# Adding the gates' logits one step later, and the last tile's product with v in both column halves, in an attention and expert kernel

## The chip, the cores and the metric

The kernel runs on one core of one Trainium2 chip. The metric is device time in microseconds (us): the median of the runs shown. All times in a trace are us from the start of the span of one profiled execution. The engines are TensorE (PE, with its weight loads PEld), VectorE (DVE), ScalarE (ACT), GpSimd (POOL) and the DMA queues, here issued by SyncE (SP). Each engine runs its instructions in the order in which the program gives them, so an instruction that waits holds up all that stand behind it on its engine.

## The reference

There are two blocks: attention in which each query keeps only its 32 best keys, and a mixture of experts with one expert per token and a capacity of 80 tokens for each.

```python
# q, k, v: (8, 8, 576, 64) float32
scores = scale * np.matmul(q, k.transpose(0, 1, 3, 2))
kth = np.partition(scores, -32, axis=-1)[..., -32:-31]
scores = np.where(scores >= kth, scores, -1e9)
attn = np.exp(scores - scores.max(-1, keepdims=True))
attn = attn / (attn.sum(-1, keepdims=True) + 1e-9)
x = np.matmul(attn, v)            # then to (4608, 512): tokens x heads*dims
...
logits = x @ w_gate               # (4608, 8)
expert_idx = np.argmax(logits, axis=1)
gate_w = softmax(logits)[expert_idx]
# for each expert e: of its tokens keep the 80 with the largest gate_w
out[tok_idx] = gate_w[tok_idx, None] * (np.maximum(x[tok_idx] @ w1[e], 0) @ w2[e])
```

## The kernel before

**Tiling.** The 64 pairs of batch and head are taken two heads at a time: 32 head pairs n, of which four (hp = 0 to 3) make a batch. The 576 queries of a head are four full tiles of 128 (t = 0 to 3) and a last tile of 64 (t = NF = 4). A full tile of a head pair is two units, one for each head. The last tiles of both heads share one unit, head 0 in partitions 0 to 63 and head 1 in 64 to 127. So a head pair has 9 units, and there are 288 in all.

**The order.** The order of all instructions of the attention is written out by hand, in `run`. Its `step(i)` issues the work for unit i and for the units a few steps before it:

- DVE: the search for the 32nd best score. `parts` finds candidates (L241); `search` takes the best of them (L252, L260) and, after y, the exact threshold (L266, L269). y is the product of scores and signs (L264), on DVE for even units and on POOL for odd ones. A step also holds the reciprocals of finished row sums (`over`, L351), which are the last of its DVE work from the letter list (L459).
- ACT: the sign of scores less a bound (L257), the mask for odd units (L278; POOL makes it for even ones, L280), the exponential (L323, L325), the division by the row sums (`divide`, L360), and copies of scores out of PSUM (L233).
- PE: scores of a unit four steps ahead (`front`, L226), transposes with the mask added (`turn_w`, L316 and L321), and the product of the weights with v (`back`, L339), in the order that the lower part of `step` gives.

**The product with v.** `back` multiplies the transposed exponentials wT of a unit with vb, which holds v and a column of ones, so that the 65th column is the row sum. The output is 128 rows of PSUM. Each matmul fills 64 of them, from one half of the array's columns (r = 0 or 64); the two halves of a full tile take the same v. For the last tile the rows number 64 for each head. Here both heads' products go to rows 0 to 63, in different columns of the PSUM tile:

```python
for r in range(0, m, TL):
    r0 = r if t < NF else TL * h
    nc.tensor.matmul(cc[r : r + TL, o], lhsT=wT[:, ..., r0 : r0 + TL], rhs=vb[:, c, h, :], ...)
```

**The gates' logits.** When a head pair is done, `norm` stores its rows to memory (L369, L371), transposes them (L201), copies the result (L377), multiplies with two heads' rows of w_gate (L382), copies the product out of PSUM (L389), and adds it on DVE to the logits of the batch (L392). Only the first head pair of a batch needs no addition. `norm` is a generator: each `yield` ends what one step issues of it. The yield's value says whether the next part needs PE (1), in which case it is put off while a step has other PE work, or not (0). Generators are advanced at the end of a step (L505), so what they put on DVE stands behind that step's search and reciprocals and ahead of the next step's. After the last head pair of each second batch `gates` follows (L403 to L426), in four parts of one step each: maximum, exponential on ACT, the chosen expert, and its weight, kept in R.

After the attention, `route` picks the tokens of each expert from R, and `finish` computes the experts.

Of the kernel before, what the change touches and what calls it, by code (L numbers as in the profile page):

```python
# [14 lines left out]
Act = mybir.ActivationFunctionType  # L15
# [12 lines left out]
def kernel(  # L28
# [11 lines left out]
    nc = tc.nc  # L40
    B, H, S, D = q.shape
# [7 lines left out]
    scale = 1.0 / math.sqrt(D)  # L49
    P = 128  # L50
    HP = H // 2
    NP = B * HP
    NF = S // P
    TL = S - NF * P
# [94 lines left out]
    class Attention:  # L149
# [178 lines left out]
        def back(self, n, t):  # L328

            wT, cc = self.w.pop((n, t))  # L330
            vb = self.vb[n % len(self.vb)]
            m = P if t < NF else TL
            for h in range(2):
                o = slice(2 * P + h * (D + 1), 2 * P + (h + 1) * (D + 1))
                j = h if t < NF else 0
                for c in range(NK):
                    for r in range(0, m, TL):
                        r0 = r if t < NF else TL * h
                        nc.tensor.matmul(cc[r : r + TL, o], lhsT=wT[:, j * NF + c if c < NF else 2 * NF + j, r0 : r0 + TL],  # L339
                                         rhs=vb[:, c, h, :], start=(c == 0), stop=(c == NF))  # L340
            self.w[n, t] = cc

        def over(self, n, t):


            m = P if t < NF else TL
            sums = self.w[n, t][:m, 2 * P : 2 * P + 2 * (D + 1)].rearrange("p (h d) -> p h d", h=2)[:, :, D]
            z = self.z[:m, n % NP, t, :]
            if self.lean:
                nc.vector.tensor_scalar(z, sums, EPS, None, op0=Alu.add)  # L350
            nc.vector.reciprocal(z, z if self.lean else sums)  # L351

        def divide(self, n, t):
            m = P if t < NF else TL
            if t == 0:
                self.xn[n] = self.rows.tile([P, NK, 2, D], F32, name="xn", tag="xn")
            cc = self.w.pop((n, t))
            for h in range(2):
                o = 2 * P + h * (D + 1)
                nc.scalar.activation(self.xn[n][:m, t, h, :], cc[:m, o : o + D], Act.Copy, scale=self.z[:m, n % NP, t, h : h + 1])  # L360

        def norm(self, n, b, hp, bi, nb, cs=range(NK)):


            xn = self.xn[n].rearrange("p c h d -> p c (h d)")
            one, cols = bass.ds(b, 1), slice(hp * P, (hp + 1) * P)
            full = [c for c in cs if c < NF]
            if full:
                nc.sync.dma_start(xv[one, : NF * P, cols].rearrange("o (c p) d -> p (o c) d", p=P), xn[:, :NF, :])  # L369
            if NF in cs:  # L370
                nc.sync.dma_start(xv[one, NF * P :, cols].rearrange("o p d -> p o d"), xn[:TL, NF:, :])  # L371
            yield 1
            ps = self.four()[:, :2, :].rearrange("p j c -> p (j c)")
            at = slice(cs[0] * P, min(S, cs[-1] * P + P))
            self.turn_in(ps, xn, cs)
            xT = self.xT
            nc.scalar.copy(xT[:, at], ps[:, at])  # L377
            yield 1
            lp = self.four()[:, 0, : NK * E].rearrange("p (c e) -> p c e", e=E)
            for c in cs:  # L380
                for r in range(0, P, TL):
                    nc.tensor.matmul(lp[r : r + TL, c, :], lhsT=xT[:, c * P + r : c * P + r + TL], rhs=wg[:, hp, :],  # L382
                                     start=True, stop=True)
            if bi == 0 and hp == 0:
                self.lg = self.small.tile([P, nb, NK, E], F32, name="lg", tag="lg", bufs=2)
            cs = slice(cs[0], cs[-1] + 1)
            lg = self.lg[:, bi, cs]
            part = lg if hp == 0 else self.small.tile([P, NK, E], F32, name="part", tag="part", bufs=2)[:, cs]
            nc.scalar.copy(part, lp[:, cs])  # L389
            yield 0  # L390
            if hp > 0:
                nc.vector.tensor_tensor(out=lg, in0=lg, in1=part, op=Alu.add)  # L392
            if hp == HP - 1 and bi == nb - 1 and cs.stop == NK:
                yield 0
                yield from self.gates(b - bi, nb)
# [32 lines left out]
        def run(self, slow):  # L428
# [17 lines left out]
            def step(i, last):  # L446
# [39 lines left out]
                if rest:  # L486
                    back()
# [12 lines left out]
                if not rest:  # L500
                    back()
# [413 lines left out]
```

## Time and profile before

| what | us |
|---|---|
| median of 6 runs | 999.73 (996.47 to 1001.67) |
| profiled execution, its own time | 999.04 |
| its span | 997.3 |

The span falls into these stages, by a table of windows (busy us of each engine, and the granted clock of PE as a share of full speed):

| window | PE | DVE | ACT | POOL | PE clock |
|---|---|---|---|---|---|
| 0 to 35, loads and first units | 23.2 | 21.3 | 16.8 | 9.0 | 1.00 |
| 35 to 865, attention | 765.8 | 810.4 | 759.1 | 426.9 | 1.00 |
| 865 to 900, last unit, gates, routing | 26.5 | 20.3 | 3.0 | 1.0 | 0.79 |
| 900 to 997.3, experts | 86.6 | 11.7 | 10.6 | 15.0 | 0.97 |

A row of the timeline gives the start, the time from the first to the last end, the engine, the line, the operation, what it writes and reads, how many instructions are merged in it, and, in brackets, how long its engine sat idle before it and what ended that. Starts on one engine can lie closer than the length of an instruction, since instructions overlap in the pipeline. In the trace a float32 matmul is two records.

### The profile page before, as it was taken

To read this page: it belongs to the slowest core of one execution; us is meant where nothing else is said; L and a number is where in the kernel's file an instruction comes from. 1 tells how busy PE (TensorE), PEld (TensorE's weight loads), DVE (VectorE), ACT (ScalarE), POOL (GpSimd) and SP (SyncE) were. 2 spreads that over 40 slices of the span, in tenths; PEclk is the share of its full clock that TensorE was granted. 3 is DMA by queue.
4 is the path that set the end of the run, shared out by engine and by line. 5 is a ranking of instruction groups with operands and counts; after the bars stand their busy time and mean duration, and the time that the engine had idled before them with its cause. 6 is when DMAs were issued, how large, how long until landed. Compare 5 with 4: busy or idle time off the path is not lost.

```text
span 997.3 us, 35583 instructions
## 1 busy us (share of the span) xinstructions
PE 902.1 (90%) x13368; PEld 724.1 (73%) x13368; DVE 863.7 (87%) x5072; ACT 789.4 (79%) x1652; POOL 451.8 (45%) x330
## 2 busy tenths in 40 slices
PE   5899999999899999999899999998999999679996
PEld 3677777777777777777677777776777777568896
DVE  5899999999999999999999999999999999571110
ACT  3799999999889989999899999998899899600110
POOL 2445555554455545555555555454555555302111
PEclk9999999999999999999999999999999999978999
DMA  3344453333332323333333322222222100044921
GB/s 72 97 127 130 127 134 91 92 91 92 92 84 68 81 80 86 86 91 92 90 82 85 86 50 50 50 49 50 49 50 49 45 18 14 18 166 141 385 69 30
DMA packets 167893, 85.76 MB, mean 86 GB/s; under 512 B 117792, under 2 KB 154656, under 8 KB 167712
## 3 DMA queue, kind: packets, MB, share of 16 engines
q1 hardware_dynamic: 166688, 80.78, 29.2%
q0 software_dynamic: 1024, 2.62, 0.8%
q8 instruction: 107, 1.75, 0.7%
q14 instruction: 74, 0.61, 0.2%
HBM read 63.19 MB, written 20.19 MB: 84 GB/s over the span
## 4 chain that ended last, share of the span: by engine, by line
DVE 48%; PE 26%; ACT 19%; issue 5%; DMA 1%; POOL 0%; POOLq 0%; SPq 0%; ACTq 0%; DVEq 0%
DVE cand L241 15%; DVE w L266 11%; DVE cand L260 6%; DVE y L264 6%; PE cc L339 5%; ACT wT L325 4%; ACT sign L257 4%; PE sp L201 4%; PE yp L799 4%; DVE top L252 4%; ACT s L233 3%; ACT mask L278 3%; PE sp L226 3%; PE ab L316 3%; DVE pick L269 2%
## 5 line engine op out<-in xcount | busy, mean ns | idle before, releaser
L241 DVE MAX8 cand<-s 128x8 f32<-128x96 f32 x1728 | 388.2, 245 | 8.9 <-ACT s L233 8.9
L280 POOL TENSOR_SCALAR mask<-s,thr_all 128x576 bf16<-128x576 f32 x144 | 248.2, 1724 | 152.0 <-DVE pick L269 117.0
L264 POOL TENSOR_TENSOR y<-s,sign 128x576 f32<-128x576 f32 x144 | 184.8, 1283 | 273.3 <-DVE pick L269 124.1
L339 PEld LDWEIGHTS cc<-vb,wT 128*64 128x64 f32 x5760 | 199.3, 138 | 104.4 <-ACT wT L325 91.7
L339 PE MATMUL cc<-vb,wT 128*64 128x65 f32 x5760 | 221.6, 224 | 33.9 <-ACT wT L325 32.3
L257 ACT ACTIVATE sign<-s,w 128x576 bf16<-128x576 f32 x288 | 225.4, 783 | 24.2 <-DVE w L252 23.8
L266 DVE MAX8 w<-y 128x8 f32<-128x576 f32 x288 | 216.2, 751 | 3.7 <-POOL y L264 3.7
L226 PE MATMUL sp<-both 64*128 64x288 f32 (+1 forms) x1280 | 202.1, 435 | 15.0 <-ACT part L389 6.5
L233 ACT ACTIVATE s<-sp 128x1152 f32<-128x1152 f32 (+1 forms) x161 | 166.9, 1037 | 12.5 <-PE sp L226 12.5
L316 PE MATMUL ab<-ident,s 128*128 128x128 f32 x1148 | 175.2, 281 | 0.0
L325 ACT ACTIVATE wT<-ab 128x1024 f32<-128x1024 f32 (+1 forms) x159 | 148.9, 937 | 0.0
L226 PEld LDWEIGHTS sp<-both 64*128 64x128 f32 (+1 forms) x1280 | 105.6, 179 | 53.8 <-ACT part L389 8.5
L316 PEld LDWEIGHTS ab<-ident,s 128*128 128x128 f32 x1148 | 127.3, 141 | 11.5 <-issue 0.9
L321 PEld LDWEIGHTS <-mask 128*128 128x128 bf16 x1440 | 93.3, 98 | 34.9 <-POOL mask L280 18.9
L252 DVE MAX8 top<-cand 128x8 f32<-128x48 f32 x576 | 114.6, 199 | 0.0
L278 ACT ACTIVATE mask<-s,thr_all 128x576 bf16<-128x576 f32 x144 | 112.5, 781 | 0.0
L260 DVE MATCH_REPLACE8 cand<-top,cand 128x48 f32<-128x48 f32 x576 | 110.3, 191 | 0.1
L264 DVE TENSOR_TENSOR y<-s,sign 128x576 f32<-128x576 f32 x144 | 106.6, 740 | 1.3 <-ACT sign L257 0.8
L360 ACT ACTIVATE xn<-cc,z_all 128x64 f32<-128x64 f32 (+1 forms) x320 | 83.0, 318 | 1.3 <-DVE z_all L351 1.3
L316 PE MATMUL cc<-ident,s 128*128 128x128 f32 x288 | 78.8, 274 | 0.0
L323 ACT ACTIVATE wT<-cc 128x256 f32<-128x256 f32 (+1 forms) x160 | 56.6, 354 | 22.2 <-PE cc L321 21.5
L269 DVE SCALAR_TENSOR_TENSOR pick<-past,cnt,w 128x9 f32<-128x9 f32 x288 | 61.5, 214 | 0.0
(188 smaller groups left out, 962.3 us busy)
## 6 DMA issues: line engine op xcount, KB each, us to landing
w<-in_moe_w_dram SPq DMA_DIRECT2D x32, 512.0 KB, 4.5
w<-in_moe_w_dram SPq DMA_DIRECT2D x8, 2048.0 KB, 12.5
out_dram<-zero SPq DMA_DIRECT2D x9, 1024.0 KB, 6.5
qn<-in_q_dram SPq DMA_DIRECT2D x64, 128.0 KB, 2.5
kn<-in_k_dram SPq DMA_DIRECT2D x64, 128.0 KB, 2.5
vb<-in_v_dram SPq DMA_DIRECT2D x64, 128.0 KB, 2.5
xd<-xn SPq DMA_DIRECT2D x32, 256.0 KB, 4.2
qn<-in_q_dram SPq DMA_DIRECT2D x32, 32.0 KB, 2.3
```

The lines of the kernel that those rows point to most:

```text
L226: nc.tensor.matmul(o, lhsT=qT[d, t * P : t * P + m], rhs=kT[d, j * HS : (j + 1) * HS], start=True, stop=True)
L233: nc.scalar.activation(s[:, j * HS : (j + w) * HS].rearrange("p (j c) -> p j c", c=HS), ps[:, j : j + w, :HS], Act.Copy, scale=TINY)
L241: nc.vector.max(out=cand[:, j, :], in_=s[:, j * S // NG : (j + 1) * S // NG])
L252: nc.vector.max(out=dst, in_=cand)
L257: nc.scalar.activation(sign, s, Act.Sign, bias=w9[:, 7:8], scale=-1.0, accum_out=cnt)
L260: nc.vector.match_replace(out=cand, in_to_replace=dst, in_values=cand, imm_value=LOW)
L264: engine.tensor_tensor(out=y, in0=s, in1=sign, op=Alu.mult)
L266: nc.vector.max(out=w9[:, 8:], in_=y)
L280: nc.gpsimd.tensor_scalar(self.mask[i], self.s[i], self.thr[:, i : i + 1], None, op0=Alu.is_lt)
L316: nc.tensor.matmul(dst[h][c], lhsT=sc[:, keys[c]], rhs=ident, start=c == 0 or (c == NF and h == 0), stop=False, is_transpose=True, skip_gr ...
L325: nc.scalar.activation(wT[:, : g * NF, :], ab.rearrange("p h c r -> p (h c) r")[:, : g * NF, :], Act.Exp, scale=scale / TINY)
L339: nc.tensor.matmul(cc[r : r + TL, o], lhsT=wT[:, j * NF + c if c < NF else 2 * NF + j, r0 : r0 + TL], rhs=vb[:, c, h, :], start=(c == 0), ...
```

## The change

Three things are done.

- In `back`, the last tile of the second head goes to rows 64 to 127 of the PSUM tile and to the same columns as the first head's, so that its matmuls alternate between the two column halves, head 0 in the one and head 1 in the other. The number of matmuls is the same, 10.
- `over` and `divide` follow: one reciprocal over 128 rows and one column in place of 64 rows and two; the division of head 1 reads rows 64 to 127 and still writes rows 0 to 63 of xn.
- In `norm`, a second `yield 0` stands between the copy of the logits out of PSUM (L389) and their addition (L392). So the addition, and `gates` where it follows, is issued one step later.

```diff
-            m = P if t < NF else TL
-            for h in range(2):
+            for h in range(2 if t < NF else 1):
                 o = slice(2 * P + h * (D + 1), 2 * P + (h + 1) * (D + 1))
-                j = h if t < NF else 0
                 for c in range(NK):
-                    for r in range(0, m, TL):
-                        r0 = r if t < NF else TL * h
-                        nc.tensor.matmul(cc[r : r + TL, o], lhsT=wT[:, j * NF + c if c < NF else 2 * NF + j, r0 : r0 + TL],
-                                         rhs=vb[:, c, h, :], start=(c == 0), stop=(c == NF))
+                    for r in range(0, P, TL):
+                        nc.tensor.matmul(cc[r : r + TL, o], lhsT=wT[:, h * NF + c if c < NF else 2 * NF + h, r : r + TL],
+                                         rhs=vb[:, c, h if t < NF else r // TL, :], start=(c == 0), stop=(c == NF))
             self.w[n, t] = cc
 
         def over(self, n, t):
...
-            m = P if t < NF else TL
-            sums = self.w[n, t][:m, 2 * P : 2 * P + 2 * (D + 1)].rearrange("p (h d) -> p h d", h=2)[:, :, D]
-            z = self.z[:m, n % NP, t, :]
+            g = 2 if t < NF else 1
+            sums = self.w[n, t][:, 2 * P : 2 * P + 2 * (D + 1)].rearrange("p (h d) -> p h d", h=2)[:, :g, D]
+            z = self.z[:, n % NP, t, :g]
...
         def divide(self, n, t):
-            m = P if t < NF else TL
...
             for h in range(2):
-                o = 2 * P + h * (D + 1)
-                nc.scalar.activation(self.xn[n][:m, t, h, :], cc[:m, o : o + D], Act.Copy, scale=self.z[:m, n % NP, t, h : h + 1])
+                if t < NF:
+                    p, o, j, m = slice(0, P), 2 * P + h * (D + 1), h, P
+                else:
+                    p, o, j, m = slice(TL * h, TL * h + TL), 2 * P, 0, TL
+                nc.scalar.activation(self.xn[n][:m, t, h, :], cc[p, o : o + D], Act.Copy, scale=self.z[p, n % NP, t, j : j + 1])
...
             nc.scalar.copy(part, lp[:, cs])
             yield 0
+            yield 0
             if hp > 0:
                 nc.vector.tensor_tensor(out=lg, in0=lg, in1=part, op=Alu.add)
```

## The prediction

> **What bounds the kernel now.** I read the page first. In its slices the attention stage (about 35 to 865 us of the span) has VectorE (DVE) at 9 tenths or more throughout, ScalarE (ACT) and TensorE (PE) just below.
>
> ```profile
> span 997.3 us, 35583 instructions
> PE 902.1 (90%) x13368; PEld 724.1 (73%) x13368; DVE 863.7 (87%) x5072; ACT 789.4 (79%) x1652; POOL 451.8 (45%) x330
> ```
>
> So a microsecond of that stage is saved only where DVE stops waiting. Next I read what DVE waited for. The columns after the colon are the total in us, the number of waits, and the longest.
>
> ```profile
> DVE lg L392 <- ACT part L389: 15.0, 16, 2.0
> ...
> DVE w L266 <- POOL y L264: 3.7, 3, 1.3
> ...
> DVE y L264 <- ACT sign L257: 0.8, 2, 0.4
> ```
>
> The one wait that recurs is the addition of the logits, L392. In the timeline of DVE it is 0.86 to 0.87 us at 14 places (105.75, 158.18, 210.51, 262.94 and so on to 792.58, one for each odd head pair), 12.1 us, and twice in the tail at 870.6 and 871.7 (1.97 and 0.93). The nine other additions, such as that at 131.89, find their operand ready.
>
> Then the chain that ended last, from 84 us on (start, length, what): it leaves DVE at 87.54, runs through ACT and PE alone for 26 us, and returns to DVE at 114.04. After that DVE paces itself until 140.12, where the pattern starts again.
>
> ```profile
> 87.54 0.12 DVE w L252
> ...
> 105.53 0.20 ACT part L389
> 105.73 0.04 issue
> 105.77 1.19 PE sp L226 x8
> 106.96 1.31 PE cc L339 x20
> ...
> 113.81 0.21 ACT sign L257
> 114.01 0.02 issue
> 114.04 0.76 DVE y L264
> ```
>
> So in half of each 52.4 us the ACT/PE chain is as late as DVE, and this chain goes through the last tile's product with v (the x20 at 106.96). The reader should see two meeting points: DVE waits at 105.75 for the copy on ACT, and at 114.04 for the sign on ACT. Taking away the first alone only moves the wait to the second.
>
> **The product, by its cost.** A table of windows (window, its length, PE busy and records, weight loads busy and records, granted clock, DMA share, GB/s) with L339 alone:
>
> ```profile
> 102.43:103.75 1.32, 1.32 (x40) 1.25 (x40) 1.00 0.06 16
> 106.89:108.20 1.31, 1.31 (x20) 1.24 (x20) 1.00 0.00 0
> ```
>
> A full tile has 20 matmuls (two records each), going to column halves 0 and 1 in turn: 40 records in 1.32 us, 33 ns each. The last tile's 10 matmuls all go to half 0: 20 records in 1.31 us, 65 ns each. The change makes them alternate too. At 33 ns, 20 records take 0.66 us, 0.65 less. Alternating with a different moving operand in each half, as the new code does, is in no row (full tiles send the same v to both halves in turn), so the bounds are 0.66 and 1.31; I take 0.66, since each record already streams by itself. There are 32 such tiles, 20.8 us of PE time, but only those on a late chain count.
>
> [...]
>
> **The addition one step later.** Same instruction, same count; the order of PE and POOL is unchanged. On DVE it moves from behind one tile's reciprocal (L351) to behind the next one's, 2.6 to 3.3 us later, when its operand has long been written (the longest regular wait was 0.87). The gates' steps (L403 to L426, three times in the stage and once in the tail) move a step with it, as does their exponential on ACT; in SP's queue three v loads, used two head pairs later, change places with a store. I cost these at nothing: both are covered by the 26 us in which DVE paces itself.
>
> What DVE gains at one place, in the regular case:
>
> ```profile
> 104.65 1.28 POOL L264 TENSOR_TENSOR y<-s,sign 128x576 f32<-128x576 f32 x1 [2.92 <-DVE cand L241]
> 104.73 0.15 DVE L351 RECIPROCAL z_all<-cc 128x2 f32<-128x2 f32 x1
> 105.75 0.23 DVE L392 TENSOR_TENSOR lg<-lg,part 128x40 f32<-128x40 f32 x1 [0.87 <-ACT part L389]
> 105.90 0.25 DVE L241 MAX8 cand<-s 128x8 f32<-128x96 f32 x1
> 106.55 0.75 DVE L266 MAX8 w<-y 128x8 f32<-128x576 f32 x1
> ```
>
> Without the addition the L241 would follow the reciprocal after 0.07 us (as at 87.70 and 87.77), at 104.80 instead of 105.90: 1.10 earlier. But L266 at 106.55 reads the y that POOL makes until 104.65 + 1.28 = 105.93. DVE's L266 has waited for POOL before (36.79 against 35.48 + 1.28, so 0.03 after its end). So L266 goes from 106.55 to 105.96, 0.59 earlier, and 0.5 us of the gain is lost to a new wait for POOL. The addition itself, put in without a wait, costs 0.10 (131.89 to 131.99). DVE was free for L264 at 113.90: two L241 start at 113.58, and the step from such a pair to an L264 that waits for nothing is 0.32 (265.13 to 265.45). It is now free at 113.90 - 0.59 + 0.10 = 113.41.
>
> ACT's side of that meeting: the sign it waits for ended at 114.01. The chain before it is shortened by the 0.65 of the product, if nothing else is late next. I checked each: ACT is free from 108.98, and its L323 moves from 109.88 to 109.23; POOL's mask for the matmuls at 109.62 is done at 108.52, and they move to 108.97; DVE's pick for the mask at 112.47 (112.28) moves with DVE. So the sign ends at 113.36, and L264 starts at about 113.40, not 114.04: **0.64 us, at 11 places, 7.0 us.** The two sides meet within 0.05, so neither half of the change does this alone.
>
> At the 3 places with gates (262.94, 474.25, 685.90) DVE has more to do and reaches L264 last anyway (272.22, ACT's sign ended 271.20). There the gain is DVE's own, 0.59 - 0.10 = 0.49: **1.5 us**. The gates' second part (269.18 to 269.87) moves behind L264; without it DVE would be there at 271.04, ACT at 270.55, so ACT does not bind.
>
> Once, at 667.84, DVE waits 0.22 for PE on a chain that holds an x20 product: **0.2 us**. In the tail the last x20 product (867.00) is on the chain to the end: what follows (reciprocal 868.48, division 868.68, xT 869.09, gates) moves up by **0.65**.
>
> The reciprocal over 128x1 in place of 64x2 lies between rows of 0.14 (64x2) and 0.15 (128x2): nothing. The division of head 1 now reads partitions 64 to 127 and writes 0 to 63, which no row shows; a 64x64 pair takes 0.50 now. I take no change, and bound it from above by 128x576 copies (0.64, so 0.39 more for the one instruction) and from below by nothing gained.
>
> **Sum:** 7.0 + 1.5 + 0.2 + 0.65 = 9.35. The profiled execution took 999.04 (span 997.3), giving 989.7; the median of the six is 999.73, 0.7 above it. Forecast 990.4 us.
>
> **Rivals.**
>
> 1. *The product does not get faster* (the second window's 65 ns stays). Then ACT's sign still ends at 114.01, and the wait moves from L392 to L264, whose start hardly changes: 0.02 x 11. At the gates L264 can start at 271.22 against 271.53 (272.22 less the deferred 0.69): 0.31 x 3. Together 1.1: 998.6. For it: a new pair of operands in no row. Against: the windows.
> 2. *More is gained, the POOL wait being smaller than I read.* Without it DVE gains 1.10 - 0.10 = 1.0 per place, and with ACT's 0.65 as the cap at 11 places the sum is 11 x 0.65 + 3 x 1.0 + 0.87 = 11.0: 988.7. If ACT caps nothing either, 14 x 1.0 + 0.87 = 14.9: 984.8. For it: only three waits at L266 are on the list. Against: the two start times above, and ACT's end at 114.01.
> 3. *Slower: the division across partitions.* It lies on the ACT chain (xn at 111.07, between the exponential and the next s). If head 1's division takes x longer, each of the 11 places and the tail gains 0.65 - x. With x = 0.39 it is 4.8 us in all: 994.9. From x = 0.65 on a place gains nothing, and the kernel is over 2 us slower from x = 0.95, when that 64-column instruction would take as long as the 128x1152 copy (L233, 1.15): 1001.7.
>
> **How the numbers follow.** Five of the six runs lie within 2.1 us, so about 0.2%, 2 us, can be told from no change. Forecast with its near neighbours, rival 2's first case and rival 3's small x among them (986.5 to 995): 0.81. Rival 1: 0.08. Rival 2 beyond 986.5: 0.05. A gain smaller than that of x = 0.39 but over 2 us: 0.02. Rival 3 from x = 0.95 on, slower: 0.04. So faster 0.88, same 0.08, slower 0.04. The range 986.5 to 995 holds the cases in which both halves work: its high end is the division at x = 0.39, its low end lies between rival 2's two cases.
>
> **What would show it.** Right: the wait at L392 gone but for the tail; in its place some 0.5 us at L266 for POOL's y at the same 14 places; L339's x20 windows at 0.66 us; the y at L264 within 0.05 us of ACT's sign at 11 places. Wrong: x20 windows still at 1.3 with 0.8 us waits at L264 for ACT (rival 1); no wait at L266 (rival 2); a 64x64 division over 0.3 us (rival 3). A wait of DVE that I haven't named, of 0.3 us or more at each of the 14 places, would make the sum wrong.

## The result, and the profile after

The changed kernel takes 996.39 us (median of 19 runs, 993.71 to 998.13) against 999.2 us of the kernel before (39 runs). The ratio is 0.9972 with a 95% interval of [0.9964, 0.9979]: 2.8 us faster. The forecast was 990.4, with a range from 986.5 to 995. The sign was right and the size was not: 9.35 us were forecast, less than a third of them came.

The profiled execution of the changed kernel was a long one (1000.25 us, span 998.5), so the totals of the two profiles can't be compared, but their stages can. The attention ends (start of the last addition) at 869.17 in place of 871.74. From there to the end of the span it took 129.4 us in place of 125.6, with a granted PE clock of 0.93 between 900 and 940 us where the kernel before had 0.97. The change touches nothing there.

First the waits of DVE in the changed kernel (total in us, times, longest):

```profile
DVE y L264 <- ACT sign L257: 4.5, 13, 0.4
DVE lg L392 <- ACT part L388: 3.3, 2, 2.2
...
DVE w L266 <- POOL y L264: 2.5, 2, 1.3
```

The wait at the addition is gone but for the two in the tail. A new one stands at y, for ACT's sign: 0.32 to 0.34 us at exactly the 11 places where the prediction had both engines meet within 0.05 (the other two of the 13 are in the first units, at 23.05 and 30.61, as in the kernel before). Of the waits at L266 for POOL, which the prediction wanted at 14 places, there is none at these places: the two in the list are at 28.38 and 36.53, in the first units. Next the product with v, alone, in a table of windows of the changed kernel (window, length, PE busy and records, weight loads, granted clock, DMA share, GB/s):

```profile
102.23:103.55 1.32, 1.32 (x40) 1.19 (x40) 1.00 0.06 16
106.63:107.36 0.73, 0.73 (x20) 0.66 (x20) 1.00 0.00 0
```

The last tile's 20 records take 0.73 us where they took 1.31, beside an unchanged 1.32 for the 40 of a full tile: 0.58 gained. Now the place where the addition stood, in the timeline of the changed kernel:

```profile
104.38 1.28 POOL L264 TENSOR_TENSOR y<-s,sign 128x576 f32<-128x576 f32 x1 [2.90 <-DVE cand L241]
104.48 0.15 DVE L348 RECIPROCAL z_all<-cc 128x2 f32<-128x2 f32 x1
104.55 0.24 DVE L241 MAX8 cand<-s 128x8 f32<-128x96 f32 x1
...
105.04 0.64 DVE L269 SCALAR_TENSOR_TENSOR pick<-past,cnt,w 128x9 f32<-128x9 f32 x1
...
105.69 0.76 DVE L266 MAX8 w<-y 128x8 f32<-128x576 f32 x1
```

L241 follows the reciprocal after 0.07 us, and L266 starts 0.03 after the end of POOL's y (104.38 + 1.28 = 105.66), both as predicted. But DVE is not idle before L266: the loss lies inside pick (L269), which is 0.64 us long where it was 0.20, as the row of the kernel before shows:

```profile
106.41 0.20 DVE L269 SCALAR_TENSOR_TENSOR pick<-past,cnt,w 128x9 f32<-128x9 f32 x1
```

Over the whole kernel the mean of pick went from 214 to 238 ns. Last, the end of the chain of waits between the two meeting points, in the changed kernel (start, length, what):

```profile
106.70 0.73 PE cc L336 x20
...
110.54 0.29 ACT xn L359
110.83 0.04 issue
110.87 1.13 ACT s L233
112.00 0.03 issue
112.03 0.78 ACT mask L278
...
113.59 0.76 DVE y L264
```

The chain still runs through ACT and PE, and in it xn, s and mask follow each other with gaps: none starts before the one ahead of it has ended. The timeline of ACT shows that this is new. Before:

```profile
110.16 1.02 ACT L325 ACTIVATE wT<-ab 128x1024 f32<-128x1024 f32 x1
111.07 0.50 ACT L360 ACTIVATE xn<-cc,z_all 64x64 f32<-64x64 f32 x2
111.46 1.12 ACT L233 ACTIVATE s<-sp 128x1152 f32<-128x1152 f32 x1
112.47 0.78 ACT L278 ACTIVATE mask<-s,thr_all 128x576 bf16<-128x576 f32 x1
113.14 0.78 ACT L257 ACTIVATE sign<-s,w 128x576 bf16<-128x576 f32 x1
```

And the same stretch of ACT in the changed kernel:

```profile
109.32 1.02 ACT L325 ACTIVATE wT<-ab 128x1024 f32<-128x1024 f32 x1
110.22 0.62 ACT L359 ACTIVATE xn<-cc,z_all 64x64 f32<-64x64 f32 x2
110.87 1.13 ACT L233 ACTIVATE s<-sp 128x1152 f32<-128x1152 f32 x1
112.03 0.78 ACT L278 ACTIVATE mask<-s,thr_all 128x576 bf16<-128x576 f32 x1
112.71 0.76 ACT L257 ACTIVATE sign<-s,w 128x576 bf16<-128x576 f32 x1
```

From the exponential to the sign it was 113.14 - 110.16 = 2.98 us and is 112.71 - 109.32 = 3.39: **0.41 us lost**, 0.12 inside the pair of divisions (0.50 to 0.62 long), 0.14 from the pair's end to s, 0.15 from s to mask. No single instruction is longer by more than 0.01 (the mean of a 64x64 division went from 302 to 305 ns). What is lost is the overlap of neighbours: before, s starts 0.11 before the pair has ended, and mask 0.11 before s has. So of the product's 0.58 us only 0.17 reach the sign. From the end of the DVE instruction that releases the chain's first sign to y it was 87.66 to 114.04 = 26.38 us, and is 87.41 to 113.59 = 26.18: 0.20 gained where 0.64 was forecast.

### The profile page after: what moved, and what is told of

Its sections match the earlier page's. It is cut to its first block, busy times and chain, and to the rows that moved or that the text cites. A ratio compares the mean times of both kernels' runs of the same rounds, so it can differ in the third digit from the quotient of the medians.

```text
span 998.5 us, 35590 instructions
## 1 busy us (share of the span) xinstructions
PE 889.1 (89%) x13368; PEld 708.9 (71%) x13368; DVE 870.5 (87%) x5072; ACT 796.1 (80%) x1652; POOL 451.3 (45%) x330
## 4 chain that ended last, share of the span: by engine, by line
DVE 55%; PE 25%; ACT 15%; issue 4%; DMA 0%; SPq 0%; POOL 0%; POOLq 0%; ACTq 0%; DVEq 0%
DVE cand L241 18%; DVE w L266 12%; DVE cand L260 7%; DVE y L264 7%; PE cc L336 6%; ACT wT L325 4%; PE yp L799 4%; DVE top L252 4%; PE sp L201 3%; ACT sign L257 3%; DVE pick L269 3%; PE sp L226 2%; ACT mask L278 2%; PE ab L316 2%; ACT s L233 2%
## 5 line engine op out<-in xcount | busy, mean ns | idle before, releaser
L241 DVE MAX8 cand<-s 128x8 f32<-128x96 f32 x1728 | 389.6, 246 | 8.8 <-ACT s L233 8.7
L280 POOL TENSOR_SCALAR mask<-s,thr_all 128x576 bf16<-128x576 f32 x144 | 247.9, 1722 | 145.6 <-DVE pick L269 122.4
L264 POOL TENSOR_TENSOR y<-s,sign 128x576 f32<-128x576 f32 x144 | 184.6, 1282 | 276.9 <-DVE pick L269 128.1
L336 PEld LDWEIGHTS cc<-vb,wT 128*64 128x64 f32 x5760 | 181.5, 138 | 111.5 <-ACT wT L325 98.7
L336 PE MATMUL cc<-vb,wT 128*64 128x65 f32 x5760 | 203.8, 225 | 40.8 <-ACT wT L325 39.0
L266 DVE MAX8 w<-y 128x8 f32<-128x576 f32 x288 | 217.0, 753 | 2.5 <-POOL y L264 2.5
L264 DVE TENSOR_TENSOR y<-s,sign 128x576 f32<-128x576 f32 x144 | 106.9, 742 | 4.5 <-ACT sign L257 4.5
L359 ACT ACTIVATE xn<-cc,z_all 128x64 f32<-128x64 f32 (+1 forms) x320 | 86.2, 317 | 1.4 <-DVE z_all L348 0.8
L269 DVE SCALAR_TENSOR_TENSOR pick<-past,cnt,w 128x9 f32<-128x9 f32 x288 | 68.6, 238 | 0.2 <-DVE z_all L348 0.2
```

The costliest lines, as they stand in the source:

```text
L241: nc.vector.max(out=cand[:, j, :], in_=s[:, j * S // NG : (j + 1) * S // NG])
L264: engine.tensor_tensor(out=y, in0=s, in1=sign, op=Alu.mult)
L266: nc.vector.max(out=w9[:, 8:], in_=y)
L280: nc.gpsimd.tensor_scalar(self.mask[i], self.s[i], self.thr[:, i : i + 1], None, op0=Alu.is_lt)
L336: nc.tensor.matmul(cc[r : r + TL, o], lhsT=wT[:, h * NF + c if c < NF else 2 * NF + h, r : r + TL], rhs=vb[:, c, h if t < NF else r // TL, ...
```

## The experiments

Each kernel is read by three numbers beside its time: the 13 periods (start of the first to start of the last addition at a place with an odd head pair and a wait before, 105.75 to 792.58 in the kernel before), the idle time of DVE before y at the 11 regular places (none: under 0.02 us), and the start of the last addition as the end of the attention. These three come from one profile of each kernel. The ratios go by the kernel before as timed beside each group: 999.22 us for e1 to e4, 999.26 for e5 to e8, 998.04 for e9 to e12. e6 and e11 were timed once and have no interval.

| kernel | 13 periods | wait at y | attention ends | us | ratio to before, 95% |
|---|---|---|---|---|---|
| before | 686.83 | 0.05 | 871.74 | 999.2 | |
| the change | 683.84 | 0.33 | 869.17 | 996.39 | 0.9972 [0.9964, 0.9979] |
| e1 addition later only | 687.02 | 0.52 | 871.67 | 998.15 | 0.9996 [0.9983, 1.001] |
| e2 halves only | 685.37 | none | 869.11 | 996.8 | 0.998 [0.9965, 0.9994] |
| e3 both divisions read rows 0-63 | 679.87 | none | 863.54 | 992.18 | 0.9935 [0.9915, 0.9954] |
| e4 one division over 128 rows | 679.90 | none | 863.39 | 994.24 | 0.9955 [0.9936, 0.9973] |
| e5 two divisions, none crosses | 684.49 | 0.35 | 868.65 | 999.66 | 1.0012 [0.9994, 1.003] |
| e6 head 1's division first | 682.54 | 0.21 | 866.86 | 994.4 | |
| e7 e4, addition at its old step | 685.80 | none | 870.41 | 998.76 | 0.9992 [0.9982, 1.0001] |
| e8 e4, max over y later | 679.05 | none | 862.15 | 993.37 | 0.993 [0.991, 0.995] |
| e9 e4, pick and max later | 678.46 | 0.12 | 864.34 | 991.88 | 0.9932 [0.991, 0.9955] |
| e10 e4, one store | 680.11 | none | 865.35 | 992.75 | 0.9947 [0.993, 0.9965] |
| e11 both divisions read rows 64-127 | 684.20 | 0.36 | 867.19 | 992.35 | |
| e12 e9 and e10 together | 678.84 | 0.11 | 862.37 | 990.48 | 0.9922 [0.99, 0.9944] |

**The two halves of the change, each alone.** e1 is the kernel before with the second yield, and nothing else:

```diff
             nc.scalar.copy(part, lp[:, cs])
             yield 0
+            yield 0
```

> The addition one step later, the product as before. Theory (ACT's chain is the second limit): the wait at L392 goes, but the y of L264 still waits for ACT's sign, so a regular place (from the DVE instruction that frees ACT's sign at the start of the chain to that y, 26.38 us before) stays at 26.3 to 26.4, with some 0.4 us of DVE idle at L264; the gates' places gain 0.3; in all 0.5 to 1.5 us: ratio 0.9985 to 0.9995. Rival (the addition alone was the limit, and the product brought nothing): the whole gain of the changed kernel, ratio 0.997.

Measured: no difference in time clear of noise, and next to none in the length of the periods (0.19 us over all 13). The wait at the addition is gone, and all that DVE gained stands at y, as a row of e1's timeline shows:

```profile
113.73 0.76 DVE L264 TENSOR_TENSOR y<-s,sign 128x576 f32<-128x576 f32 x1 [0.52 <-ACT sign L257]
```

e2 is the changed kernel without that yield, so only the product, reciprocal and division are new.

> The product in both halves and the division across partitions, the addition as before. Theory: DVE still waits 0.87 at L392, so only the 0.14 that DVE waited at L264 can be won at 11 places, and some at the tail: 1 to 2.5 us, ratio 0.9975 to 0.999. The pair of divisions of the last tile is followed by the next ACT instruction 0.64 us after its start, not 0.39 to 0.40. Rival (the product alone carries the gain): ratio 0.997, with the wait at L392 shorter than 0.87.

Measured: the addition waits as before (0.85 to 0.87 us at the 14 places), and a period is 1.46 / 13 = 0.11 us shorter. That is the distance by which DVE, free at 113.90, was ahead of ACT's sign at 114.01 in the kernel before. So the two meeting points that the prediction read out of the chain are real: one half of the change moves the wait, the other gains the 0.11 us until DVE is the later one. In time, though, e2 (996.8) can't be told from the whole change (996.39): as long as the divisions cost what they do, the second yield adds 685.37 - 683.84 = 1.53 us over the 13 periods, which the times don't resolve. The attention ends of the two agree (869.11 and 869.17), since e2's profile is ahead before its first period, which starts at 105.0 in place of 105.75 (a wait of 1.18 us at L266 among the first units, at 36.79 in the kernel before, is missing), and the changed kernel lost time in its tail (see the last part of the next section).

**The division.** e3 takes out what no row of the trace before had shown, an instruction of ACT that reads partitions 64 to 127. Head 1's rows of the last tile are left out for it; head 0's stand in their place:

```diff
-                    p, o, j, m = slice(TL * h, TL * h + TL), 2 * P, 0, TL
+                    p, o, j, m = slice(0, TL), 2 * P, 0, TL
```

> The changed kernel, but the division of head 1's last tile reads rows 0 to 63 (head 0's product and row sums) in place of 64 to 127, so that part of x is head 0's. Theory (ACT loses about 0.4 us at each last tile because an instruction that reads 64 to 127 and writes 0 to 63 does not overlap its neighbours): the next ACT instruction starts 0.39 to 0.40 us after the pair, the mask after s 1.01 and not 1.16; a regular place takes 25.75 to 25.9 us in place of 26.18, so the kernel is some 4 to 5 us faster than the changed one: ratio to the kernel before 0.991 to 0.9935. Rival (ACT is held by something else, such as PE or its order against DVE): no difference to the changed kernel, ratio 0.997.

Measured: everything that was lost comes back. ACT's stretch in e3:

```profile
109.54 1.02 ACT L325 ACTIVATE wT<-ab 128x1024 f32<-128x1024 f32 x1
110.44 0.50 ACT L359 ACTIVATE xn<-cc,z_all 64x64 f32<-64x64 f32 x2
110.83 1.12 ACT L233 ACTIVATE s<-sp 128x1152 f32<-128x1152 f32 x1
111.85 0.78 ACT L278 ACTIVATE mask<-s,thr_all 128x576 bf16<-128x576 f32 x1
112.51 0.78 ACT L257 ACTIVATE sign<-s,w 128x576 bf16<-128x576 f32 x1
```

From the exponential to the sign it is 2.97 us again, no wait is left at y, and the attention ends 8.2 us earlier than before. e4 keeps the computation and gets there in another way: xn holds the last tile of both heads as 128 rows, divided by one instruction, and its rows are stored by two DMAs and transposed by two matmuls of 64 rows.

```diff
-            for h in range(2):
...
+            for h in range(2 if t < NF else 1):
+                o = 2 * P + h * (D + 1)
+                nc.scalar.activation(self.xn[n][:, t, h, :], cc[:, o : o + D], Act.Copy, scale=self.z[:, n % NP, t, h : h + 1])
```

> The changed kernel with one division of 128 rows for both heads of the last tile, each head staying in its own partitions; the turning back happens in PE (two 64-row matmuls with the identity in place of one transpose) and in two stores of 64 columns. Theory: ACT gains 0.2 us more than in the run without the crossing, since one instruction goes; PE takes 0.1 to 0.3 more in the turn of x (L201), which lies on the chain; DVE's side (POOL's y) caps a regular place at 25.75, so 25.75 to 26.0: ratio 0.991 to 0.9935. Rival: as in the changed kernel, 0.997, if the partitions of the division don't matter.

Measured: the same attention as e3, within 0.2 us at its end. But from there to the end of the span e4 takes 128.1 us and e3 125.4, and with that the ratio, 0.9955, lies outside the 0.991 to 0.9935 that was expected.

**Crossing, or starting at partition 64?** Up to here I held the crossing (reading 64 to 127, writing 0 to 63) for the cause. e5 cuts e4's one division in two that stay in their partitions:

```diff
-                nc.scalar.activation(self.xn[n][:, t, h, :], cc[:, o : o + D], ...)
+                for r in (slice(0, P),) if t < NF else (slice(0, TL), slice(TL, P)):
+                    nc.scalar.activation(self.xn[n][r, t, h, :], cc[r, o : o + D], ...)
```

> The kernel of e4_one_div with its one 128x64 division of the last tile cut in two 64x64 divisions, each of which reads and writes the same partitions (0 to 63, then 64 to 127). Theory (what ACT loses at the division in the changed kernel comes from the one instruction that reads partitions 64 to 127 and writes 0 to 63): from the start of the pair to the start of s 0.39 us as in the kernel before (0.65 in the changed kernel), from s to mask 1.01 to 1.03 (1.16 in the changed kernel), no wait of DVE at y for ACT's sign at the 11 regular places, and the attention as long as in e4_one_div: 679.9 us from the first to the last addition of such a place, 994 to 995 in all. Rival (any instruction that starts at partition 64 beside one that starts at 0 costs it, crossing or not): pair to s 0.6 to 0.7, s to mask 1.15, a wait of 0.3 us at each of the 11 places, 683 to 684 over the 13 periods, 996.5 to 998.

Measured: my theory fell and its rival held. ACT in e5, which crosses nowhere, loses just what the changed kernel loses:

```profile
109.02 1.02 ACT L325 ACTIVATE wT<-ab 128x1024 f32<-128x1024 f32 x1
109.92 0.64 ACT L357 ACTIVATE xn<-cc,z_all 64x64 f32<-64x64 f32 x2
110.58 1.13 ACT L233 ACTIVATE s<-sp 128x1152 f32<-128x1152 f32 x1
111.74 0.78 ACT L278 ACTIVATE mask<-s,thr_all 128x576 bf16<-128x576 f32 x1
112.42 0.76 ACT L257 ACTIVATE sign<-s,w 128x576 bf16<-128x576 f32 x1
```

112.42 - 109.02 = 3.40 us, and 0.35 of wait at y. So the price, 3.40 - 2.98 = 0.42 us here, goes with the partition at which a division starts and not with the crossing. (The time, 999.66, is above the 996.5 to 998 of the rival too: behind the attention e5 takes 128.8 us, more on that below.) e6 is the changed kernel with the two divisions in the other order:

```diff
-            for h in range(2):
+            for h in range(2) if t < NF else (1, 0):
```

> The changed kernel with the two divisions of the last tile in the other order: head 1's, which crosses from partitions 64-127 to 0-63, comes first and head 0's after it. The question is which neighbours lose their overlap. If only the instruction right behind the crossing one does: the second division starts 0.3 us or more after the first, and s comes 0.39 or less behind the pair's usual spacing, s to mask back at 1.01 to 1.03, and the wait at y for ACT's sign falls from 0.33 to 0.1 to 0.2 us. If what follows stays slow for several instructions whatever their place (as pair to s +0.26 and s to mask +0.15 in the changed kernel): 0.65 and 1.15 again, wait 0.3 us, 683 to 684 us over the 13 periods. One look, total about as the changed kernel.

e11 lets both divisions read the upper half, so that head 0's rows are the ones left out:

```diff
-                    p, o, j, m = slice(TL * h, TL * h + TL), 2 * P, 0, TL
+                    p, o, j, m = slice(TL, P), 2 * P, 0, TL
```

> The changed kernel with both divisions of the last tile reading partitions 64 to 127 (head 1's product twice) and writing 0 to 63, so that head 0's rows hold head 1's: the counterpart of e3_no_cross, which read 0 to 63 twice. Theory (ACT loses 0.12 to 0.15 us wherever the partition that an instruction starts reading at differs from that of the one before, whether it crosses or not): no loss inside the pair, 0.50 long as in e3; 0.14 to 0.15 lost before it (wT to pair 1.05 in place of 0.90), 0.13 behind it (pair to s 0.52 in place of 0.39), and at the mask 0.15 as in e5 (1.16 in place of 1.01). Rival (an instruction that reads the upper partitions is itself slower or blocks its follower): the pair 0.62 or more as well. The wait at y 0.3 us and 683 to 684 over the 13 periods either way.

Measured, the rows of e6 first:

```profile
109.59 1.02 ACT L325 ACTIVATE wT<-ab 128x1024 f32<-128x1024 f32 x1
110.64 0.63 ACT L359 ACTIVATE xn<-cc,z_all 64x64 f32<-64x64 f32 x2
111.17 1.11 ACT L233 ACTIVATE s<-sp 128x1152 f32<-128x1152 f32 x1
112.19 0.76 ACT L278 ACTIVATE mask<-s,thr_all 128x576 bf16<-128x576 f32 x1
112.85 0.77 ACT L257 ACTIVATE sign<-s,w 128x576 bf16<-128x576 f32 x1
```

And those of e11:

```profile
108.10 1.02 ACT L325 ACTIVATE wT<-ab 128x1024 f32<-128x1024 f32 x1
109.15 0.51 ACT L359 ACTIVATE xn<-cc,z_all 64x64 f32<-64x64 f32 x2
109.68 1.13 ACT L233 ACTIVATE s<-sp 128x1152 f32<-128x1152 f32 x1
110.84 0.78 ACT L278 ACTIVATE mask<-s,thr_all 128x576 bf16<-128x576 f32 x1
111.52 0.76 ACT L257 ACTIVATE sign<-s,w 128x576 bf16<-128x576 f32 x1
```

In e6 the loss stands ahead of the pair (1.05 from the exponential in place of 0.91) and inside it (0.63), while s and mask have their old distances (s starts 0.10 before the pair's end, and mask 1.02 after s): two neighbours lose, 3.26 - 2.98 = 0.28 us, and the wait at y falls to 0.21. In e11 the pair is whole (0.51), and the loss stands ahead of it (1.05), behind it (s starts 0.02 after its end) and at the mask (1.16): three neighbours, 3.42 - 2.98 = 0.44. The instruction that reads the upper partitions is not slower in itself (the pair takes 0.51 in e11, where both do); in these kernels each change of the starting partition costs an overlap, 0.12 to 0.15 us. That the mask loses one too in three of the four kernels, though s lies between, is taken up below. It is not the mask's own: at the other last tiles a sign follows s in its place, and in the changed kernel that sign loses as much (136.55 to 137.71, 1.16 us from s; in the kernel before 137.20 to 138.21, 1.01).

**Are both halves needed once ACT is free?** e7 is e4 with the addition back at its old step.

> The kernel of e4_one_div with the addition back at its old step: the product's halves and one division without a crossing, and no later addition. Theory (both halves of the change are needed, each takes away the wait that the other leaves): the addition waits again for ACT's part at 14 places, by less than the 1.10 us of the kernel before, since part comes some 0.6 to 0.7 us earlier by the product and the division: 0.4 to 0.5 us of DVE's time each, 13 x 0.4 to 0.5 = 5 to 6.5 us over e4_one_div's 679.9, so 685 to 686.5, and 998 to 999.5 in all. Rival (DVE has enough other work queued, so that the crossing alone was the matter): as e4_one_div, 680 and 994.

Measured: both are. The time is that of the kernel before, the periods 0.08 us shorter each, and the wait at the addition 0.89 us. I had expected 0.4 to 0.5, since the product is faster; that was wrong, because the copy that the addition waits for (105.56 in e7) follows PE's product with w_gate (104.83 + 0.71 = 105.54 in the chain of waits), and PE makes that one ahead of the last tile's product (106.93), so it gains nothing from it.

**What holds pick?** e8 is e4 with the max over POOL's y (L266, the letter g) two DVE instructions later, with pick left at its place:

```diff
-                for c in "ghmGbGycGdGGGeaz" if i % 2 else "GbGhmgcGdGeGGyaz":
+                for c in "ghmGbGycGdGGGeaz" if i % 2 else "GbGhmcGgdGeGGyaz":
```

> The kernel of e4_one_div with one step of the even pattern put one place later: the step that issues DVE's max over POOL's y comes one step of the other search later, so DVE has some 0.5 us more of its own work before it needs that y. Theory (with the crossing gone, the place's length is DVE's own work with the wait for POOL's y in it, shown as a pick of 0.57 to 0.64 us instead of 0.21): pick falls to 0.21 to 0.35 us at the 14 places, and each place gains up to 0.35 to 0.4 us until ACT's sign is met again; 13 x 0.2 to 0.4 = 2.6 to 5 us less than 679.9, 990 to 992 in all. Rival (the same step in the other places of the pattern has no wait and now loses: POOL's mask, and the product behind it, come a step later): 682 or more over the 13 periods, 996 or more in all.

Measured, POOL and DVE in e8:

```profile
103.90 1.28 POOL L264 TENSOR_TENSOR y<-s,sign 128x576 f32<-128x576 f32 x1 [2.92 <-DVE cand L241]
...
104.54 0.66 DVE L269 SCALAR_TENSOR_TENSOR pick<-past,cnt,w 128x9 f32<-128x9 f32 x1
...
105.13 0.20 DVE L252 MAX8 top<-cand 128x8 f32<-128x48 f32 x1
105.25 0.24 DVE L241 MAX8 cand<-s 128x8 f32<-128x96 f32 x1
105.41 0.74 DVE L266 MAX8 w<-y 128x8 f32<-128x576 f32 x1
```

The 13 periods are 0.85 us shorter than e4's in all. The max now comes 0.23 us after the end of y (105.18) and waits for nothing, yet pick is as long as ever and ends with y (105.20). So pick, which reads nothing of y, is itself held by POOL's instruction, and my expectation that it would shrink was wrong. In the changed kernel all 17 picks that begin while POOL makes y end 0.02 or 0.03 us after y does (0.46 to 1.28 us long); the other 271 take 0.20 to 0.23.

e9 moves pick, mask and max behind that work ("GbGcGhmgdGeGGyaz" for the even pattern).

> The kernel of e4_one_div with the even pattern's pick, mask and max over y two steps (L252 and L241, 0.35 us of DVE's work) later. e8_one_div_g moved only the max over y behind them, and pick stayed 0.66 us long and ended 0.02 us after POOL's y. Theory (pick, which reads nothing of y, can't run on DVE while POOL's tensor_tensor runs, so it is held until that ends): pick now begins at 105.4 and ends with y at 105.7 or 105.8, 0.3 us long in place of 0.66 to 0.70, and DVE has done 0.35 us more by then; each regular period is 0.2 to 0.35 us shorter until ACT's sign is met, 13 x 0.2 to 0.35 = 2.6 to 4.5 us less than 679.9, 990 to 992 in all. Rival (pick's length has to do with the addition or the step itself, and moves with it): pick 0.6 or more again, 679.9 and 994.

Measured: pick starts at 105.10, ends with y again (0.41 us long), and the 13 periods are 678.46 us, 1.4 less than e4's where 2.6 to 4.5 were expected. The stretch between two additions that holds such a pick is 0.28 us shorter (133.32 to 159.60 against 133.63 to 160.19), but the one ahead of it 0.22 longer (107.81 to 133.32, 25.51, against 25.29 in e4). There DVE meets ACT's sign again, in rows of both engines in e9:

```profile
112.42 0.40 DVE L241 MAX8 cand<-s 128x8 f32<-128x96 f32 x2
112.72 0.19 ACT L257 ACTIVATION_READ_ACCUMULATOR sign<-s,w 128x1 f32 x1
112.94 0.76 DVE L264 TENSOR_TENSOR y<-s,sign 128x576 f32<-128x576 f32 x1
```

y starts 0.52 us after the two L241 ahead of it, where e4 has 0.32 (112.94 to 113.26), and 0.03 after the sign has ended (112.72 + 0.19 = 112.91). So 0.20 of the 0.22 is a wait for ACT: the limit that the theory named ("until ACT's sign is met") came sooner than I had reckoned.

**The store, and both together.** e10 puts e4's two stores of the last tile's rows into one DMA:

```diff
-                for h in range(2):
-                    nc.sync.dma_start(xv[...hp * P + h * D...], xn[h * TL : h * TL + TL, NF:, :D])
+                nc.sync.dma_start(xv[one, NF * P :, cols].rearrange("o p (h d) -> (o h) p d", h=2), xn[:, NF, :D])
```

> The kernel of e4_one_div with its two stores of the last tile's rows put into one DMA over both partition halves. e4's attention ended as early as e3_no_cross's (863.39 and 863.54), but from there to the end it took 128.1 us and e3 125.4, with PE's waits without a releaser in the expert stage 2 to 3 us longer. Theory (the store that was added, 32 more DMAs in the queue, is what the expert stage's loads come late by): the rest back at 125 to 126, attention 679.9 again, 991.5 to 992.5 in all. Rival (it is the clock or the place of the program in memory, from run to run): as e4, 994.

Measured: 127.8 us from the end of the attention to the end of the span, as in e4; the theory of the extra store fell. Every kernel with the last tile in 128 rows of xn takes 126.5 to 128.8 us there, and those with the old layout 123.4 to 126.8, except the changed kernel's 129.4. Whether the layout is the cause stays open. e12 joins e9 and e10.

> e9_pick_late and e10_one_store together: if both theories hold, 2.6 to 4.5 us from the places and 2 to 3 from the expert stage below e4_one_div's 994.2: 987 to 989.5. If the store's does not hold, as e9_pick_late; if pick's does not, as e10_one_store.

Measured: 990.48 us, ratio 0.9922 [0.99, 0.9944], 7.6 us below the kernel before in the same runs (998.04) and the lowest median of the kernels that leave nothing out, though its interval overlaps those of e9 and e10. It doesn't reach the 987 to 989.5 that both theories together promised, since neither gave its whole share.

## Why the prediction was wrong, point by point

**The step that failed** is "The division of head 1 now reads partitions 64 to 127 and writes 0 to 63, which no row shows ... I take no change". It costs 0.41 us on the ACT chain, just over the upper bound of 0.39 that was worked out and set aside. Rival 3 had the place right, and its sum with the upper bound, 994.9, was the nearest of all. With the measured 0.58 - 0.41 = 0.17 a place, 11 places give 1.9 us where 7.0 were forecast. That alone is most of the missing 6.5, and e3 shows it: with nothing but that loss taken out, the attention ends 8.2 us earlier, and the time is 992.18 against 999.22 (ratio 0.9935, so 6.5 us by the ratio).

Rival 3's sign would not have shown it. It named "a 64x64 division over 0.3 us", and the division is as long as before: the cost is not in any instruction's length but in the distances between three of them, so it has to be read from start to start.

The cause the prediction gave to that rival, "the division across partitions", was not it either: e5 crosses nowhere and loses the same. The rows name the neighbours that lose their overlap one by one. In the changed kernel and e5 it is head 1's division (64 after 0), then s (0 after 64), then the mask, 1.16 us from s in place of 1.01: three, 0.41 and 0.42 us. In e6 it is both divisions, while s and the mask keep their old distances: two, 0.28. In e11 it is the first division, s and the mask: three, 0.44. In e3 none: 2.97 us as before. In e6, s stands two behind an instruction that read the upper half and is free, so it is not a matter of distance alone. The mask loses its 0.15 where the division just ahead of s reads from 64 (the changed kernel, e5, e11) and nothing where it reads from 0 (e3, e6). By what it does so, with s between the two, was not shown.

**The product**: alternating the halves brought most of what the two windows promised. The two windows of before differ in more than the column half, since the old product of the last tile also changed its moving operand with each matmul, where a full tile uses one twice; but the new one changes it each time too, and takes 0.73 us against 1.31. That is in place of the 0.66 taken, so 0.58 gained in place of 0.65. The reason given for 0.66, that each record streams by itself, was my reading of the 40 records of a full tile; what was measured is the 0.73. 40 records take 1.32 and 20 take 0.73, which, by a line through the two, is an estimate of 0.0295 each and 0.14 once; the 33 ns per record of a full tile had that 0.14 spread over twice as many.

**The addition one step later**: right at the regular places, and a little short at the others. L241 right behind the reciprocal (104.55 after 104.48; in the kernel before 105.90 after 104.73, with the waiting addition between them), L266 at 105.69 with POOL's end at 105.66, and the three double periods that hold a place with gates (two periods each, 210.51 to 317.06 the first in the kernel before) are 0.32, 0.63 and 0.93 us shorter. Less the 0.18 of the regular period in each that is 1.34, where 1.5 was forecast for these places and 0.2 for the one at 667.84, which lies in the third. What was wrong is the name of the wait: not L266 for its operand but pick for POOL's instruction, as e8 shows. L266 comes out at the same time, so the sum did not suffer. But the sign to look for, 0.5 us of idle time at L266, is not in the profile.

**The meeting of the two sides**: right, and e1, e2 and e7 show it. Each half alone gains 0 to 0.11 us a period, and both together, without the loss on ACT, 6.96 / 13 = 0.54.

**The tail**: 0.65 was forecast. In the changed kernel's profile it is 0.86 lost between the last regular y (3.43 us earlier than before) and the last addition (2.57), with a granted clock of PE of 0.74 from 852 to 857 us where the kernel before had 1.00. In e6 and e11, whose clock is 1.00 there, the stretch from the last addition of a regular place to the last of all is 75.80 and 75.96 us, and 76.44 in e1 with the old product: 0.5 to 0.6 gained, about what was forecast.

## What to carry to other kernels

Before an operand moves to other partitions, look at what stands beside the instruction on its engine: on ACT, a division whose input starts at partition 64 between neighbours that start at 0 cost up to three overlaps in these kernels, 0.12 to 0.15 us each, and no instruction's length showed it. If such an instruction can't be avoided, let its sister that starts at 0 follow it (e6: 0.28 us lost in place of 0.41), or let one instruction cover all 128 rows (e4: no wait at y, where the changed kernel has 0.33). And a change that works only if two waits go at once is worth the smaller of the two gains, so the term that no row of the profile shows decides it and belongs in the forecast's middle, not in its range.

## What the runs showed of the hardware

- A wait can lie inside an instruction. In the changed kernel DVE's pick is 0.20 to 0.23 us alone and 0.46 to 1.28 us in the 17 cases in which it begins while POOL makes y (L264), and there it ends 0.02 or 0.03 us after y does; the idle time of DVE shows nothing. Beside another instruction of POOL no such hold is seen: 130 of DVE's own y begin within the last 0.66 us of POOL's mask (L280) in the changed kernel and take 0.73 to 0.76 us as the others do.
- What follows the last addition took 123.4 (e11) to 129.4 us (the change) in the 14 profiles, although no edit changes an instruction there: the spread is twice what the change is worth. The granted clock of PE between 900 and 940 us was 0.93 in the change and 0.97 in the kernel before, and 1.00 in e3 to e6, e8 to e10 and e12; but among these lie both e3's 125.4 us and e5's 128.8, so this clock alone does not account for it. So read a change in the attention from the attention's own times, and not from the total.
